# Retention and ELU layer: the opening chunks load k in one layout and get the other by transposes

## The chip, the cores and the metric

The kernel runs on one core of one Trainium2 chip. The metric is device time in microseconds (us) for one whole execution, inputs in device memory to outputs in device memory; lower is better. Lines written L307 and the like are lines of the kernel before.

## The reference

Two blocks run one after the other. The first is a retention layer with a decaying state per head (batch 4, 8 heads, 768 tokens, head size 64). The second is a two-layer network with an ELU between the layers (3072 tokens, 512 to 2048 to 512). All data is float32.

```python
for t in range(S):
    state = gamma * state + einsum('bhd,bhe->bhde', k[:, :, t], v[:, :, t])
    y[:, :, t] = scale * einsum('bhd,bhde->bhe', q[:, :, t], state)
x = y.transpose(0, 2, 1, 3).reshape(B * S, H * D)
h = x @ w_in
g = where(h > 0, h, exp(minimum(h, 0)) - 1)
out = g @ w_out
```

## The kernel before

**Tiling.** Tokens are cut into 24 chunks of 128. Four chunks make a block of 512 tokens, and there are six blocks. Within a chunk the retention is worked out in two halves of 64 tokens: products of q and k inside each half (scores), a lower-triangular mask over them, products of the masked scores with v (the inner part of the output), the state after each half (products of k and v, summed up), and products of q with the state (the part across halves). Powers of each head's decay are put on v beforehand and on the output afterwards, so the state itself needs no decay. The network then runs on a whole block. Block 0 uses plain products for its first layer (`plain_first`); later work uses Strassen products.

**Four parts of a chunk.** A chunk is one tile of 128 x 2048 numbers (1 MB). Columns 0 to 511 hold q with head dimension on the partitions, columns 512 to 1023 hold k in the same turned layout, columns 1024 to 1535 hold k with tokens on the partitions, and columns 1536 to 2047 hold v with tokens on the partitions. Scores read both turned parts. The state products read k with tokens on the partitions, so k is loaded twice. The masked scores overwrite the turned k (`mask_pair`, L328). The sums of states overwrite the other k (`state`, `state_sum`, L348 and L350).

**Weights.** They come in pieces of 1 MB in 64-bit form (`load_piece`, L142). ScalarE makes the first step of their conversion (`prepare`: L164, L166 and, unless VectorE does it, L168), VectorE the rest (`decode`: L191 and L194, after L190 where VectorE does that step too). Piece 0 becomes the first quarter of `w_a`, piece 1 the first quarter of `w_b`, piece 2 the second quarter of `w_a`. Each of the first two is handled in two halves, and a call of `take()` issues one step of a half: a half of piece 0 takes two calls.

**Order.** Every engine runs its instructions in the order in which the program issues them; nothing is reordered by a planner. Semaphore waits are inserted by the framework from the tiles that are read and written. All loads go through SyncE's queue, in this order at the start: chunk 0 first half, chunk 0 second half, piece 0 first half, chunk 1, piece 0 second half, piece 1, chunk 2, chunk 3, piece 2. The load of piece 2 waits for a GpSimd copy (L115) that waits for piece 1.

**The opening**, from L1106 on, is written out by hand:

1. TensorE multiplies zeros (`unread`, one of 512 columns, then 28 of 64), as it does later with the other calls of `unread`. Nothing reads these results.
2. Chunk 0: scores (L307), v scaled (`scale_v`, L281), mask (L328), state products (L338), state (L348), inner output (L394), the part across halves (L409, with a tiny copy `seen`, L426, between its two orders), and the output times decay powers into `xb` (L433).
3. An `unread` of 512 columns, then the scores of chunk 1.
4. ScalarE prepares piece 0, and between its two halves fills the table of decay powers for tokens 256 to 767 (`powers_of`, L249, four instructions).
5. VectorE decodes the first half of piece 0, then scales v of chunk 1 and masks its scores.
6. TensorE runs the first layer on chunk 0 (`plain_first`, L497, first part), then the state products, inner output and across part of chunk 1; VectorE sums the states between.
7. An `unread` of 512 columns, `xb` for chunk 1, decode of the second half of piece 0, decode of piece 1, and the first layer on both chunks (L497), followed by chunks 2 and 3 and the rest of the network.

`warm` and `other` are two banks of PSUM, called `pa` and `pb` in the profile.

Of the kernel before, what the change touches and what calls it, by code (L numbers as in the profile page):

```python
# [14 lines left out]
ALU = mybir.AluOpType  # L15
# [3 lines left out]
def kernel(  # L19
# [32 lines left out]
    nc = tc.nc  # L52
    PSUM = bass.MemoryType.PSUM
    P = nc.NUM_PARTITIONS
# [3 lines left out]
    C = P  # L58
# [37 lines left out]
    chunks = [divmod(m, NCH) for m in range(NCHUNK)]  # L96
    raw = {}

    def load(m, parts=1):

        if m >= NCHUNK:
            return
        t = ldpool.tile([P, 2048], FP32, name="chunk", tag="chunk")
        raw[m] = (
            t[:, 0:1024].rearrange("p (a h c) -> p a h c", a=2, c=C),
            t[:, 1024:2048].rearrange("p (a h d) -> p a h d", a=2, d=D),
        )
        for part in range(parts):
            c = slice(part * 2048 // parts, (part + 1) * 2048 // parts)
            nc.sync.dma_start(t[:, c], qkv[m, :, c])  # L110

    def hold(t, other):

# [66 lines left out]
    def decode(fine=False):  # L180

        n = len(decoded)
        if n >= NPIECE:
            return
        dst, todo = prepared[n]
        decoded.append(dst.rearrange("p (a b) -> p a b", a=2))
        vec = nc.vector
        for c, flat, hi in todo:
            if hi is not None:
                vec.tensor_scalar(c.bitcast(FP32), hi.bitcast(FP32), 2.0**-112, None, ALU.mult)  # L190
            vec.tensor_scalar(c, c, 3, 0x7FFFFFF8, ALU.logical_shift_left, ALU.bitwise_and)  # L191
            if fine:
                yield
            vec.tensor_tensor(out=flat, in0=c, in1=flat, op=ALU.add)  # L194
# [28 lines left out]
    for h in range(H):  # L223
# [10 lines left out]
    nc.gpsimd.affine_select(  # L234
        out=causal, in_=causal, compare_op=ALU.is_gt, fill=1.0, base=0, pattern=[[-1, P]], channel_multiplier=1
    )
    cmask = const.tile([P, D], FP32, name="cmask")
    for sub in range(2):
        r = slice(sub * D, (sub + 1) * D)
# [6 lines left out]
    def powers_of(tokens):  # L246
        for a in range(2):
            for u in range(2):
                nc.scalar.activation(etab[:, a, u, tokens], post[:, tokens], AF.Exp, scale=lny[:, a, u : u + 1])  # L249

    powers_of(slice(0, 2 * C))

    load(0, 2)
    parts = load_piece_parts(2)
    next(parts)
    load(1)
    next(parts, None)
    load_piece()
    load(2)
# [15 lines left out]
    def scale_v(m, by_vector=False):  # L275
        if m >= NCHUNK:
            return
        i = chunks[m][1]
        qk, kv = raw[m]
        eng = nc.vector if by_vector or m < 2 else nc.gpsimd  # L280
        eng.tensor_tensor(  # L281
            out=kv[:, 1], in0=kv[:, 1], in1=vf[:, i].unsqueeze(2).to_broadcast([C, H, D]), op=ALU.mult
        )

    rows = lambda n: slice(n * D, (n + 1) * D)
# [1 line left out]
    def state(tb, n):  # L287

        if n % (2 * CPB) == 0:
            return carry[(tb + n // (2 * CPB)) % 2]  # L290
        if (tb, n) == (0, 3):

            return xt[0].rearrange("p a t -> p (a t)")[:, 0:256].rearrange("p (h e) -> p h e", e=D)

        k = raw[tb * CPB + (n - 1) // 2][1][:, 0].rearrange("p h d -> p (h d)")
# [6 lines left out]
    def score_products(sc, tb, pp, x):  # L302
        qk = raw[tb * CPB + 2 * pp + x][0]
        for p in range(HP):
            for sub in range(2):
                for a in range(2):
                    nc.tensor.matmul(  # L307
                        sc[a][rows(sub), x, p, :], lhsT=qk[rows(a), 1, p, rows(sub)],
                        rhs=qk[rows(a), 0, p, rows(sub)], start=True, stop=True, skip_group_check=True,
                    )  # L310
# [13 lines left out]
    def mask_pair(sc, x):  # L324

        place = raw[x][0][:, 1].rearrange("p h c -> p (h c)").rearrange("p (a n t) -> p a n t", a=2, t=D)
        for a in range(2):
            nc.vector.tensor_tensor(  # L328
                out=place[:, a], in0=sc[a][:, x], in1=cmask.unsqueeze(1).to_broadcast([P, HP, D]), op=ALU.mult
            )  # L330

    def state_products(kvs, tb, pp, x, subs):
        kv = raw[tb * CPB + 2 * pp + x][1]
        for p in range(HP):
            for sub in subs:
                for a in range(2):
                    if not fresh(tb, 4 * pp + 2 * x + sub + 1):
                        nc.tensor.matmul(  # L338
                            kvs[sub][rows(a), x, p, :], lhsT=kv[rows(sub), 0, 2 * p + a, :],
                            rhs=kv[rows(sub), 1, 2 * p + a, :], start=True, stop=True, skip_group_check=True,  # L340
                        )

    def state_sum(kvs, tb, pp, x, sub, copy=None):
        n = 4 * pp + 2 * x + sub
        if fresh(tb, n + 1):
            return
        if fresh(tb, n):
            (copy or nc.scalar.copy)(state(tb, n + 1), kvs[sub][:, x])  # L348
        else:
            nc.vector.tensor_tensor(out=state(tb, n + 1), in0=kvs[sub][:, x], in1=state(tb, n), op=ALU.add)  # L350
# [38 lines left out]
    def within(tb, pp, x, j, y, pt):  # L389
        kv = raw[tb * CPB + 2 * pp + x][1]  # L390
        a, u = divmod(j, 2)
        for sub in range(2):
            for c in range(2):
                nc.tensor.matmul(  # L394
                    y[sub][rows(c), j, x, :], lhsT=kv[rows(sub), 1, head(a, u, c), :], rhs=pt(2 * u + c)[rows(sub)],
                    start=(x == 0 and j == 0), stop=False, skip_group_check=True,
                )

# [702 lines left out]

    warm, other = (bank(x).rearrange("p a b -> p (a b)") for x in "ab")

    def unread(count, n):
        for _ in range(count):
            nc.tensor.matmul(warm[:, 0:n], lhsT=blank[:, 0:P], rhs=blank[:, 0:n], start=True, stop=True, skip_group_check=True)  # L1106

    unread(1, TB)
    for n in range(28):
        nc.tensor.matmul(  # L1110
            (warm, other)[n % 2][rows(n // 2 % 2), 0:D], lhsT=blank[rows(n % 2), 0:D], rhs=blank[rows(n % 2), 0:D],
            start=True, stop=True, skip_group_check=True,
        )
    sc = [ps_r.tile([P, 2, HP, D], FP32, name="sc", tag="r") for _ in range(2)]
    score_products(sc, 0, 0, 0)
    scale_v(0)
    mask_pair(sc, 0)
    unread(1, TH)
# [369 lines left out]
```

## Time and profile before

| what | value |
|---|---|
| time, median of 3 runs | 632.92 us (632.59 to 634.07) |
| the profiled execution: its time | 632.87 us |
| its span | 630.9 us |
| TensorE matmul busy | 624.8 us, 99% of the span |
| VectorE busy | 483.1 us, 77% |
| ScalarE busy | 253.3 us, 40% |
| GpSimd busy | 21.8 us, 3% |

The span runs from the first to the last instruction of the profiled execution; its own time is 1.97 us longer. In the profile, PE is TensorE's matmul side and PEld its weight load side, DVE is VectorE, ACT is ScalarE, POOL is GpSimd, SP is SyncE. A float32 matmul leaves two records, each with its own weight load, so 16 score products of one chunk are 32 records. A row of the timeline has the start, the time it covers, the engine, the line, the operation, and output and inputs with their shapes; in brackets stands the idle time before it and what ended that. The end of a matmul record is modelled and includes the time the result takes to come out, so records of neighbouring matmuls overlap.

### The profile page before, as it was taken

To read this page: it belongs to the slowest core of one execution; us is meant where nothing else is said; L and a number is where in the kernel's file an instruction comes from. 1 tells how busy PE (TensorE), PEld (TensorE's weight loads), DVE (VectorE), ACT (ScalarE), POOL (GpSimd) and SP (SyncE) were. 2 spreads that over 40 slices of the span, in tenths; PEclk is the share of its full clock that TensorE was granted. 3 is DMA by queue.
4 is the path that set the end of the run, shared out by engine and by line. 5 is a ranking of instruction groups with operands and counts; after the bars stand their busy time and mean duration, and the time that the engine had idled before them with its cause. 6 is when DMAs were issued, how large, how long until landed. Compare 5 with 4: busy or idle time off the path is not lost.

```text
span 630.9 us, 16128 instructions
## 1 busy us (share of the span) xinstructions
PE 624.8 (99%) x6680; PEld 560.1 (89%) x6680; DVE 483.1 (77%) x884; ACT 253.3 (40%) x472; POOL 21.8 (3%) x25
## 2 busy tenths in 40 slices
PE   8999999999999999999999999999999999999998
PEld 5864578888899999889999989999988999988997
DVE  5779789989789675699685588777489877558975
ACT  6698635015541114653112646111465211366311
POOL 1021000000000000200000200000110000000000
PEclk9999999999999999999999999999999999999999
DMA  8698669689287888405888702888810798600794
GB/s 331 278 406 291 188 210 268 196 267 316 81 311 248 239 255 299 180 2 174 274 266 292 282 2 64 264 284 296 310 73 12 216 308 252 217 18 2 232 309 162
DMA packets 75897, 136.85 MB, mean 217 GB/s; under 512 B 6320, under 2 KB 31792, under 8 KB 70704
## 3 DMA queue, kind: packets, MB, share of 16 engines
q1 hardware_dynamic: 75824, 135.82, 64.8%
q8 instruction: 53, 0.87, 0.5%
q14 instruction: 20, 0.16, 0.1%
HBM read 114.56 MB, written 21.23 MB: 215 GB/s over the span
## 4 chain that ended last, share of the span: by engine, by line
PE 77%; SPq 1%; DVE 1%; DMA 1%; issue 0%; ACT 0%; ACTq 0%; DVEq 0%
PE pa L955 20%; PE pa L913 10%; PE pd L955 10%; PE pb L955 5%; PE pa L867 5%; PE pb L913 4%; PE pa L740 4%; PE qa L913 3%; PE pd L867 2%; PE qd L913 2%; PE pd L913 2%; PE pd L740 2%; PE y L394 1%; PE sc L307 1%; PE y L409 1%; PE kv L338 1%
## 5 line engine op out<-in xcount | busy, mean ns | idle before, releaser
L963 ACT COPY ms<-pa 128x128 f32<-128x128 f32 x104 | 27.7, 266 | 146.7 <-PE pa L955 146.7
L955 PE MATMUL pa<-ts,wq 128*128 128x128 f32 x560 | 74.2, 275 | 0.0
L955 PE MATMUL pd<-ts,wq 128*128 128x128 f32 x552 | 73.5, 276 | 0.0
L955 PEld LDWEIGHTS pa<-ts,wq 128*128 128x128 f32 x560 | 68.5, 192 | 0.4
L955 PEld LDWEIGHTS pd<-ts,wq 128*128 128x128 f32 x552 | 67.1, 192 | 0.6 <-DVE res L967 0.2
L955 PE MATMUL pa<-gC,wq 128*128 128x128 f32 x480 | 64.7, 278 | 0.0
L478 ACT ACTIVATE r<-r 128x512 f32<-128x512 f32 x96 | 60.5, 630 | 3.1
L955 PEld LDWEIGHTS pa<-gC,wq 128*128 128x128 f32 x480 | 59.0, 192 | 1.5 <-issue 0.3
L477 ACT ACTIVATE r<-gC 128x512 f32<-128x512 f32 x64 | 39.9, 624 | 32.4 <-DVE gC L921 32.4
L967 DVE TENSOR_TENSOR res<-pd,ms 128x128 f32<-128x128 f32 x68 | 19.5, 287 | 39.6 <-PE pd L955 38.4
L481 DVE SCALAR_TENSOR_TENSOR gC<-r,gC 128x512 f32<-128x512 f32 x64 | 44.0, 719 | 0.7 <-ACT r L478 0.7
L829 DVE TENSOR_TENSOR ts<-gC,ts 128x512 f32<-128x512 f32 x60 | 41.3, 688 | 1.0
L829 DVE TENSOR_TENSOR ts<-gC 128x512 f32<-128x512 f32 x60 | 41.0, 684 | 0.0
L281 POOL TENSOR_TENSOR chunk<-chunk,vf 128x512 f32<-128x512 f32 x16 | 20.0, 1251 | 428.8 <-DMA chunk<-in_qkv_dram 345.8
L955 PE MATMUL pb<-gC,wq 128*128 128x128 f32 x240 | 31.7, 275 | 0.0
L988 ACT COPY res<-pa 128x128 f32<-128x128 f32 x34 | 9.0, 266 | 55.0 <-PE pa L955 55.0
L955 PEld LDWEIGHTS pb<-gC,wq 128*128 128x128 f32 x240 | 29.2, 192 | 0.0
L690 ACT COPY m<-pa 128x512 f32<-128x512 f32 x24 | 13.9, 581 | 30.2 <-PE pa L740 16.3
L921 DVE TENSOR_TENSOR gC<-qa,gC 128x512 f32<-128x512 f32 x8 | 5.5, 692 | 25.0 <-PE qa L913 18.3
L913 PE MATMUL pa<-xt,w_b 128*128 128x256 f32 x96 | 23.0, 382 | 0.0
L913 PE MATMUL pa<-xt,w_s 128*128 128x256 f32 x96 | 23.0, 382 | 0.0
L913 PE MATMUL pa<-xb,w_a 128*128 128x256 f32 x96 | 22.7, 379 | 0.0
(255 smaller groups left out, 1244.3 us busy)
## 6 DMA issues: line engine op xcount, KB each, us to landing
wq<-scratch_dram SPq DMA_DIRECT2D x277, 256.0 KB, 4.3
chunk<-in_qkv_dram SPq DMA_DIRECT2D x23, 1024.0 KB, 8.6
wraw<-in_w_dram SPq DMA_DIRECT2D x15, 1024.0 KB, 6.0
out_dram<-res SPq DMA_DIRECT2D x14, 256.0 KB, 3.8
scratch_dram<-gT SPq DMA_DIRECT2D x12, 256.0 KB, 4.3
scratch_dram<-m SPq DMA_DIRECT2D x12, 192.0 KB, 6.0
scratch_dram<-so SPq DMA_DIRECT2D x4, 512.0 KB, 4.6
scratch_dram<-wi SPq DMA_DIRECT2D x2, 1024.0 KB, 6.4
```

The costliest lines, as they stand in the source:

```text
L281: eng.tensor_tensor(out=kv[:, 1], in0=kv[:, 1], in1=vf[:, i].unsqueeze(2).to_broadcast([C, H, D]), op=ALU.mult)
L477: nc.scalar.activation(e, h, AF.Relu, scale=-1.0)
L478: nc.scalar.activation(e, e, AF.Exp, scale=-1.0)
L481: nc.vector.scalar_tensor_tensor(g, e, -1.0, h, ALU.add, ALU.max)
L690: nc.scalar.copy(m, ps)
L740: nc.tensor.matmul(ps[:, fi, :], lhsT=w[:, fi, j2, :], rhs=x[:, j2, :], start=(begin and fi == 0 and j2 == 0), stop=(j2 == 1), skip_group_ ...
L829: sub = lambda o, x, y: nc.vector.tensor_tensor(out=o, in0=x, in1=y, op=ALU.subtract)
L867: nc.tensor.matmul(ps[:, f, :], lhsT=lhs[f], rhs=xs[j][k], start=(begin and f == 0), stop=True, skip_group_check=True,)
L913: nc.tensor.matmul(ps[:, fi, :], lhsT=w[:, fi, j2, :], rhs=x[:, j2, :], start=(j in (1, 7) and fi == 0 and j2 == 0), stop=(j2 == 1), skip_ ...
L955: nc.tensor.matmul(ps, lhsT=w[:, f, :], rhs=ts[j][k][:, f, :], start=(begin and f == 0), stop=(f == 3), skip_group_check=True,)
L963: nc.scalar.copy(m, ps)
L967: nc.vector.tensor_tensor(out=o, in0=x, in1=y, op=ALU.add)
```

## The change

The plain part of a chunk swaps its order on the host: v now takes columns 1024 to 1535, k with tokens on the partitions 1536 to 2047. All indices of the two follow.

For chunks 0 and 1 the last 512 columns are not loaded. Chunk 0 comes as 1024 and 512 columns (it was 1024 and 1024), chunk 1 as 1536 (it was 2048). Their k with tokens on the partitions is made on the core: four transposes on TensorE per chunk (`turn`, one per pair of heads, against an identity matrix that GpSimd builds with two new instructions) into the bank `warm`, and one ScalarE copy of 128 x 512 from there into columns 1536 to 2047 (`turned`).

In the opening, 28 multiplications of zeros become 24. The transposes of a chunk follow its scores. The `unread` of 256 columns now stands between the transposes of chunk 0 and its state products and writes `other`; the `unread` of 512 columns ahead of the scores of chunk 1 is gone. On VectorE the scaling and masking of chunk 1 come ahead of the decode of piece 0's first half, and so does the state after chunk 0; that decode now stands between `seen` and `xb` of chunk 1. The first part of the first layer moves behind the last `unread`. On ScalarE the copy `turned` of chunk 1 takes the place of `powers_of` between the halves of piece 0, and `powers_of` comes after piece 1.

```diff
-    def load(m, parts=1):
+    def load(m, cuts=(0, 2048)):
...
-        for part in range(parts):
-            c = slice(part * 2048 // parts, (part + 1) * 2048 // parts)
-            nc.sync.dma_start(t[:, c], qkv[m, :, c])
+        for lo, hi in itertools.pairwise(cuts):
+            nc.sync.dma_start(t[:, lo:hi], qkv[m, :, lo:hi])
...
+    identity = begin[:, 2 * S + P : 2 * S + 2 * P]
+    nc.gpsimd.memset(identity, 0.0)
+    nc.gpsimd.affine_select(
+        out=identity, in_=identity, compare_op=ALU.not_equal, fill=1.0, base=0, pattern=[[-1, P]], channel_multiplier=1
+    )
...
-    load(0, 2)
+    load(0, (0, 1024, 1536))
     parts = load_piece_parts(2)
     next(parts)
-    load(1)
+    load(1, (0, 1536))
...
+    def turn(m, ps):
+
+        for p in range(HP):
+            nc.tensor.transpose(ps[:, p * P : (p + 1) * P], raw[m][0][:, 1, p, :], identity)
+
+    def turned(m, ps):
+
+        nc.scalar.copy(raw[m][1][:, 1].rearrange("p h d -> p (h d)"), ps)
+
...
     unread(1, TB)
-    for n in range(28):
+    for n in range(24):
...
     score_products(sc, 0, 0, 0)
+    turn(0, warm)
+    unread(1, TH, other)
+    turned(0, warm)
     scale_v(0)
     mask_pair(sc, 0)
-    unread(1, TH)
     kvs = [ps_r.tile([P, 2, HP, D], FP32, name="kv", tag="r") for _ in range(2)]
     state_products(kvs, 0, 0, 0, range(2))
     state_sum(kvs, 0, 0, 0, 0, nc.vector.tensor_copy)
     y = outputs_of_first()
     next(y)
     next(y)
-    unread(1, TB)
     score_products(sc, 0, 0, 1)
-    state_sum(kvs, 0, 0, 0, 1)
-    prepare(2, between=lambda: powers_of(slice(2 * C, S)))
-    piece = decode(True)
-    take()
-    take()
+    turn(1, warm)
     scale_v(1)
     mask_pair(sc, 1)
-    inner = plain_first()
-    next(inner)
+    state_sum(kvs, 0, 0, 0, 1)
+    prepare(2, between=lambda: turned(1, warm))
+    piece = decode(True)
     state_products(kvs, 0, 0, 1, range(2))
     state_sum(kvs, 0, 0, 1, 0)
     next(y)
     next(y)
+    take()
+    take()
     next(y)
     unread(1, TB)
+    inner = plain_first()
+    next(inner)
     next(y, None)
     take()
     take()
     take()
     state_sum(kvs, 0, 0, 1, 1)
     prepare(2, by_vector=True)
+    powers_of(slice(2 * C, S))
     next(inner)
...
-    plain = [x.reshape(B, H, NC, C, D).transpose(0, 2, 3, 1, 4).reshape(B * NC, C, H * D) for x in (k, v)]
+    plain = [x.reshape(B, H, NC, C, D).transpose(0, 2, 3, 1, 4).reshape(B * NC, C, H * D) for x in (v, k)]
```

More of the change, by code (lines that the diff above doesn't have):

```diff
@@ L278, in scale_v @@
         i = chunks[m][1]
-        qk, kv = raw[m]
+        v = raw[m][1][:, 0]
         eng = nc.vector if by_vector or m < 2 else nc.gpsimd
         eng.tensor_tensor(
-            out=kv[:, 1], in0=kv[:, 1], in1=vf[:, i].unsqueeze(2).to_broadcast([C, H, D]), op=ALU.mult
+            out=v, in0=v, in1=vf[:, i].unsqueeze(2).to_broadcast([C, H, D]), op=ALU.mult
         )
@@ L293, in state @@
             return xt[0].rearrange("p a t -> p (a t)")[:, 0:256].rearrange("p (h e) -> p h e", e=D)
-        k = raw[tb * CPB + (n - 1) // 2][1][:, 0].rearrange("p h d -> p (h d)")
+        k = raw[tb * CPB + (n - 1) // 2][1][:, 1].rearrange("p h d -> p (h d)")
         return k[:, (n - 1) % 2 * 256 : ((n - 1) % 2 + 1) * 256].rearrange("p (h e) -> p h e", e=D)
@@ L338, in state_products @@
                         nc.tensor.matmul(
-                            kvs[sub][rows(a), x, p, :], lhsT=kv[rows(sub), 0, 2 * p + a, :],
-                            rhs=kv[rows(sub), 1, 2 * p + a, :], start=True, stop=True, skip_group_check=True,
+                            kvs[sub][rows(a), x, p, :], lhsT=kv[rows(sub), 1, 2 * p + a, :],
+                            rhs=kv[rows(sub), 0, 2 * p + a, :], start=True, stop=True, skip_group_check=True,
                         )
@@ L394, in within @@
                 nc.tensor.matmul(
-                    y[sub][rows(c), j, x, :], lhsT=kv[rows(sub), 1, head(a, u, c), :], rhs=pt(2 * u + c)[rows(sub)],
+                    y[sub][rows(c), j, x, :], lhsT=kv[rows(sub), 0, head(a, u, c), :], rhs=pt(2 * u + c)[rows(sub)],
                     start=(x == 0 and j == 0), stop=False, skip_group_check=True,
@@ L1102, with unread @@
     warm, other = (bank(x).rearrange("p a b -> p (a b)") for x in "ab")
-    def unread(count, n):
+    def unread(count, n, to=warm):
         for _ in range(count):
-            nc.tensor.matmul(warm[:, 0:n], lhsT=blank[:, 0:P], rhs=blank[:, 0:n], start=True, stop=True, skip_group_check=True)
+            nc.tensor.matmul(to[:, 0:n], lhsT=blank[:, 0:P], rhs=blank[:, 0:n], start=True, stop=True, skip_group_check=True)
     unread(1, TB)
-    for n in range(28):
+    for n in range(24):
         nc.tensor.matmul(
```

## The prediction

> **What bounds the kernel now.** I read the page first, for the share of each engine.
>
> ```profile
> span 630.9 us, 16128 instructions
> ...
> PE 624.8 (99%) x6680; PEld 560.1 (89%) x6680; DVE 483.1 (77%) x884; ACT 253.3 (40%) x472; POOL 21.8 (3%) x25
> ```
>
> TensorE is idle for 6.1 us of 630.9. Next, the view of waits for TensorE's matmul side: who made it wait in the whole span.
>
> ```profile
> PE pa L1106 <- DVE blank L208: 1.5, 1, 1.5
> PE pd L409 <- DVE seen L426: 0.5, 2, 0.3
> PE kv L338 <- DVE chunk L281: 0.4, 1, 0.4
> PE y L409 <- DVE seen L378: 0.3, 1, 0.3
> PE pa L497 <- DVE w_a L194: 0.2, 1, 0.2
> ```
>
> All of these lie in the first 28 us, and busy time by stretch is full from 30 to 140 us. So the rest is a queue of TensorE work, and a shift of where it starts goes to the end nearly one for one. But the opening's "busy" holds multiplications of zeros, so its real waits must be read in the timeline. TensorE:
>
> ```profile
> 5.15 1.06 PE L307 MATMUL sc<-chunk 64*64 64x64 f32 x32
> 6.14 0.70 PE L1106 MATMUL pa<-blank 128*128 128x256 f32 x2
> 7.21 0.69 PE L338 MATMUL kv<-chunk 64*64 64x64 f32 x32 [0.37 <-DVE chunk L281]
> ...
> 10.66 0.69 PE L307 MATMUL sc<-chunk 64*64 64x64 f32 x32
> 11.59 1.13 PE L497 MATMUL pa<-xb,w_a 128*128 128x128 f32 x8 [0.23 <-DVE w_a L194]
> 12.65 0.69 PE L338 MATMUL kv<-chunk 64*64 64x64 f32 x32
> ...
> 18.93 1.99 PE L497 MATMUL pb<-xb,w_b 128*128 128x256 f32 x8
> ```
>
> VectorE, same view:
>
> ```profile
> 11.36 0.69 DVE L281 TENSOR_TENSOR chunk<-chunk,vf 128x512 f32<-128x512 f32 x1
> 11.96 0.75 DVE L328 TENSOR_TENSOR chunk<-sc,cmask 128x256 f32<-128x256 f32 x2
> 13.38 0.42 DVE L350 TENSOR_TENSOR xt<-kv,chunk 128x256 f32<-128x256 f32 x1 [0.66 <-PE kv L338]
> ...
> 15.10 0.42 DVE L433 TENSOR_TENSOR xb<-pb,etab 128x256 f32<-128x256 f32 x1 [0.58 <-PE pb L409]
> ...
> 18.19 0.69 DVE L194 CUSTOM_DVE_ANT_0 w_b<-wraw,w_b 128x1024 uint16<-128x1024 uint16 x1
> ```
>
> (In that last row the first half of w_b is finished, at 18.88.) Chunk 1's scores wait for its load (10.66); the first layer waits for w_a, then the state products start at 12.65. From 15.10 VectorE has no gap that matters until 18.88, when TensorE can begin with w_b (18.93). After that TensorE is nearly without a gap. The opening thus ends at that 18.93, reached through 12.65.
>
> [...] No transpose is in this trace. [...] the first 32 score records take 1.06 us, the next 32 take 0.69. [...] Here the readers of successive loads start in that order, at 5.15, 6.46, 8.11, 10.66 and (piece 1) 15.06.
>
> **The change, part by part.**
>
> Loads. Chunk 0's second half took 6.46 - 5.15 = 1.31 for 512 KB; half of it saves 0.65. Chunk 1 took 10.66 - 8.11 = 2.55 for 1 MB; a quarter less saves 0.64. So v arrives at 5.81, piece 0 at 7.46, chunk 1 at 9.37, piece 1 at 13.8, piece 2 1.29 earlier than before. SyncE issues as many loads as before; the held load of piece 2 (L115) is released earlier too. [...]
>
> Transposes. Price S, first start to readable. Nearest row: eight 128x128 records take 1.13 (L497), with 0.275 for one, so each adds (1.13 - 0.275)/7 = 0.12. If a transpose leaves one record, S = 0.275 + 3 x 0.12 = 0.64, which I take. Two records each: S = 1.13[...]. [...] The copy of 128x512 from PSUM on ScalarE takes 0.58 (L690's row), with 0.05 per handoff.
>
> Chunk 0. Scores run as before, the transposes start at 6.14 and are readable at 6.78. VectorE scales v from 5.81 to 6.50. The mask overwrites the turned k, so its second half waits for all four transposes: done about 7.3 (before 7.82), harmless. Copy: 6.83 to 7.41. State products start at 7.46, where they were at 7.21 behind L281: **+0.25**. The zeros (`other`) fit into the copy's time. The chain of chunk 0 moves by 0.25, so TensorE is free at 9.51 + 0.25 = 9.76, without the `unread` that filled 9.51 to 10.64.
>
> Chunk 1. Its data is there at 9.37, so scores start at 9.76, transposes 0.56 later, the time that the weight loads of those 32 records take (10.32), readable at 10.96. ScalarE is done with piece 0's first half at 7.46 + 2.02 = 9.48, so it copies 11.01 to 11.59. VectorE leaves chunk 0 at 10.22 (9.97 + 0.25): scaling to 10.82, mask with its second half waiting for the transposes (10.96) to 11.55, then the state after chunk 0, 0.42, to 11.95. The state products write the bank that this last one reads, so beyond the first pair they wait for it, not for the copy: effective start **11.94 against 12.65, -0.71**. Queued behind it: the inner output, across part, w_a's first use.
>
> The moved decode. From the state products to the end of `seen` the sequence is the same, 1.86: 13.80 (before 14.51). In the old order the decode took 1.06 (10.30 to 11.36) ahead of the scaling; now it stands ahead of `xb`, where VectorE idled 0.58 for TensorE. So `xb` starts at 13.73 + 1.06 = 14.79 against 15.10: **-0.31**. Behind it the VectorE order is unchanged, so w_b is ready at 18.57. TensorE's side: across part done 14.25, zeros 0.86, two first-layer parts of 0.86 each and one of 1.73: 18.6 (w_a's second half, at 16.60, is in time). The two bounds agree: **-0.3**.
>
> Moved at nothing: `powers_of` (2.55) comes after piece 1 on ScalarE, 13.8 + 2.9 = 16.7 to 19.3. Its cover is ScalarE's wait of 4.87 for piece 2, now landing near 21.5; its table is first read at 27.85. If that cover went, piece 2's decode (26.95) still has slack. The first first-layer part moves behind an `unread`: counted above. GpSimd's two instructions (0.21 and 0.29 like their twins) end near 3, before 6.14. The four missing zero products (about 0.1) precede a wait for the load.
>
> Sum: 632.87 for the profiled execution (630.9 span plus 1.97 around it, untouched), minus 0.3, is **632.6**; the profiled execution lies 0.05 below the median of 632.92.
>
> Ends: [...] S = 1.13 puts scores at 10.25, transposes readable at 11.94, state at 12.75: +0.5. Loads that save only half add at most 0.3 (scores at 10.0). The first four transposes at half clock add about 0.4.
>
> **Rivals.**
>
> 1. *Transposes and copy become the wait* (a new wait for the one removed). The scores, transposes, mask and state sum stand in series, as above: S = 1.13 with slow clock or short saving, +0.5 to +1.1, 633.4 to 634.0. For it: nothing in this trace prices a transpose. Against it: two transpose groups would have to cost as much as full products.
> 2. *Slower: the clock.* Place: 6.1, where the clock has just come up, and 10.96 to 11.9, where TensorE now stands without its zeros. If the transposes don't count and the clock stays or falls to half[...], that window's work (the second chunk's products, zeros and first-layer parts, 2.3 to 3 us) takes twice its time: +2.3, about 635.2. It decides once more than 1.9 us of work on the path runs at half clock. Against it: [...] the trace kept full clock across its own waits.
> 3. *The loads were the bound, everything comes 1.29 earlier*: 631.6. Against it: VectorE's serial 1.06 decode is only moved, and TensorE's own sum reaches 18.6.
> 4. *Nothing gained*: the load is hidden, the copy eats it: 632.9.
>
> **How the numbers follow.** The forecast 0.57, rival 4 0.14, rival 1 0.18, rival 3 0.05, rival 2 0.06. A measurement of this kernel can tell about 0.3% (1.9 us) from no change; only rival 2 passes that upwards. Even rival 3 stays within it; for more than 1.9 us I know no source and leave 0.02 out of rival 3's chance. Faster 0.02, same 0.92, slower 0.06. The range holds the forecast, rivals 1 and 4, the price bounds and the runs' own spread (632.59 to 634.07): 632.0 to 634.0.
>
> **What would show it.** Right: chunk 1's scores near 9.8 without a wait for a load; state products near 12, released by VectorE's state sum after chunk 0, `xb` near 14.8, the first w_b product near 18.6. Wrong: transposes that cover over 1 us, state products of chunk 1 released by ScalarE, a second score group as slow as the first (clock), or gaps in TensorE after 19.

## The result, and the profile after

The changed kernel takes **636.3 us** (median of 7 executions, 634.94 to 638.53) against 633.01 us (7 executions, 632.59 to 634.31): ratio 1.0046, 95% interval 1.0027 to 1.0064. It is slower, by 0.46%. The forecast was 632.6 us within 632.0 to 634.0: outside, on the wrong side.

Every execution also gives TensorE's mean granted clock over the span. Four of the seven executions of the changed kernel show 0.994 or 0.995, and their median is 636.67; the other three show 1.0, median 635.35. So there are two losses: about 2.3 us that is there at full clock (635.35 - 633.01; in the second session below, where the clocks of the kernel before are on record too, it is 1.6), and more where the clock fell. The profiled execution (635.65 us, span 633.8) is one at full clock. Lines from here on are lines of the changed kernel, mostly 13 above those of before (but the scaling is L285, L281 before, and the mask L332, L328 before); experiments built on the kernel before keep its lines, and e8 and e9 have a few of their own.

The page of the changed kernel:

```profile
span 633.8 us, 16133 instructions
...
PE 624.8 (99%) x6678; PEld 560.8 (88%) x6678; DVE 483.8 (76%) x884; ACT 254.0 (40%) x474; POOL 21.0 (3%) x27
...
q8 instruction: 53, 0.87, 0.5%
```

TensorE is busy for the same 624.8 us as before; the span is 2.9 longer, all of it idle time. The view of waits says who made it wait (engine, line, what it waited for; total, times, longest):

```profile
PE pa L1119 <- DVE blank L207: 1.5, 1, 1.5
PE y L422 <- issue: 1.3, 1, 1.3
PE kv L351 <- DVE chunk L332: 0.7, 1, 0.7
PE pd L422 <- DVE seen L439: 0.5, 2, 0.3
PE pa L753 <- DVE m L608: 0.5, 1, 0.5
PE pa L753 <- ACT m L703: 0.5, 1, 0.5
```

The first and fourth were there before. The third is chunk 1's wait in the opening; the view puts it down to the mask, which is not so, as shown below. The second, fifth and sixth are new and lie far from the change: at 301.94, 134.23 and 141.92 us. The opening itself, on TensorE (start, length):

```profile
5.89 1.07 PE L339 MATMUL pa<-so,chunk 128*128 128x128 f32 x4
...
7.63 0.69 PE L351 MATMUL kv<-chunk 64*64 64x64 f32 x32 [0.24 <-ACT chunk L343]
...
10.47 0.66 PE L339 MATMUL pa<-so,chunk 128*128 128x128 f32 x4
11.80 1.20 PE L351 MATMUL kv<-chunk 64*64 64x64 f32 x29 [0.68 <-DVE chunk L332]
...
19.14 1.91 PE L510 MATMUL pb<-xb,w_b 128*128 128x256 f32 x8
...
27.57 0.67 PE L510 MATMUL hp<-xb,w_a 128*128 128x256 f32 x2
```

And on VectorE:

```profile
11.72 0.41 DVE L363 TENSOR_TENSOR chunk<-kv,chunk 128x256 f32<-128x256 f32 x1
13.08 0.42 DVE L363 TENSOR_TENSOR xt<-kv,chunk 128x256 f32<-128x256 f32 x1 [0.94 <-PE kv L351]
...
15.21 0.42 DVE L446 TENSOR_TENSOR xb<-pb,etab 128x256 f32<-128x256 f32 x1
```

State products of chunk 1 start at 11.80, but cover 1.20 where they covered 0.69. ScalarE's copy and the weight loads of these products show what they wait for:

```profile
11.16 0.58 ACT L343 COPY chunk<-pa 128x512 f32<-128x512 f32 x1 [1.69 <-PE pa L339]
```

```profile
11.80 0.20 PEld L351 LDWEIGHTS kv<-chunk 64*64 64x64 f32 x4 [0.91 <-ACT chunk L343]
12.19 0.67 PEld L351 LDWEIGHTS kv<-chunk 64*64 64x64 f32 x25 [0.20 <-DVE chunk L363]
```

The first weight load waits for a semaphore of ScalarE, so the copy, done at 11.74, releases it; the mask is no input of these products and ends at 11.81, after they have started. After the first two products, whose records start from 11.80 to 11.91, nothing starts until 12.19, when VectorE's sum of states (L363, 11.72 to 12.13) is done. A second gap, from 12.43 to 12.60, is ended by nothing that the profile shows.

`xb` comes at 15.21 (before 15.10), the first w_b product at 19.14 (18.93), and the work on `hp` at 27.57 (27.78). So at the end of the opening, at full clock, the changed kernel is ahead by no more than 0.2 us. To see where the time went, I matched TensorE's instructions of the two traces and took the median shift of after against before in stretches of before's time: -0.20 us at 27.5 to 30, 0.01 at 60 to 80 and at 110 to 130, **1.21** at 142 to 150, 1.08 at 280 to 297, **2.56** at 300 to 310, 2.56 at the end. Two steps, near 134 to 142 and near 300, make the whole loss of this execution.

**The first step, traced back.** TensorE waits at 134.23 for `m` (L608, VectorE) and at 141.92 for `m` (L703, ScalarE). Followed back, VectorE has been late since 95 us, where it makes sums of weights in the buffers of `m` and must wait until stores that read these buffers have landed in device memory. Before:

```profile
94.54 0.55 DVE L647 TENSOR_TENSOR m<-w_s 128x384 f32<-128x384 f32 x1
```

After, with a wait of 1.01 us for the stores of `m`:

```profile
95.64 0.56 DVE L660 TENSOR_TENSOR m<-w_s 128x384 f32<-128x384 f32 x1 [1.01 <-DMA scratch_dram<-m]
```

Those stores are issued by SyncE. Before:

```profile
88.32 4.30 SPq L643 DMA_DIRECT2D scratch_dram<-m  x4
```

After, starting earlier and covering 1.77 us more (6.07 - 4.30):

```profile
87.71 6.07 SPq L656 DMA_DIRECT2D scratch_dram<-m  x4
```

What else was moving then? The page's "q8 instruction" is a queue of instruction packets: 53 of 16 KB, 0.87 MB in all. The trace places each one. The reads near these stores (start in us, length in ns):

```
                before        after         one zero less (e2)   filler and count (e5)
9th read      78.94/ 880    78.63/1020      78.34/ 881           78.96/ 880
10th read     86.57/1335    92.27/ 935      92.17/ 936           86.18/1031
11th read    114.98/ 931   115.22/1195     114.61/ 931          114.75/ 938
```

The tenth read came 5.7 us later and fell among these stores. Whether that is a cause, and of what, is what half of the experiments ask.

### The profile page after: what moved, and what is told of

It reads as the page before. It is cut to its first block, busy times and chain, and to the rows that moved or that the text cites. A ratio compares the mean times of both kernels' runs of the same rounds, so it can differ in the third digit from the quotient of the medians.

```text
span 633.8 us, 16133 instructions
## 1 busy us (share of the span) xinstructions
PE 624.8 (99%) x6678; PEld 560.8 (88%) x6678; DVE 483.8 (76%) x884; ACT 254.0 (40%) x474; POOL 21.0 (3%) x27
## 4 chain that ended last, share of the span: by engine, by line
PE 77%; SPq 1%; DVE 1%; DMA 1%; issue 1%; ACT 0%; ACTq 0%; DVEq 0%
PE pa L968 20%; PE pa L926 10%; PE pd L968 10%; PE pb L968 5%; PE pa L880 5%; PE pb L926 4%; PE pa L753 4%; PE qa L926 3%; PE pd L880 2%; PE qd L926 2%; PE pd L926 2%; PE pd L753 2%; PE y L407 1%; PE y L422 1%; PE sc L311 1%; PE kv L351 1%
## 5 line engine op out<-in xcount | busy, mean ns | idle before, releaser
L285 POOL TENSOR_TENSOR chunk<-chunk,vf 128x512 f32<-128x512 f32 x16 | 18.8, 1177 | 433.8 <-DMA chunk<-in_qkv_dram 347.5
L703 ACT COPY m<-pa 128x512 f32<-128x512 f32 x24 | 13.9, 580 | 29.8 <-PE pa L753 16.0
```

The source lines that it names most:

```text
L285: eng.tensor_tensor(out=v, in0=v, in1=vf[:, i].unsqueeze(2).to_broadcast([C, H, D]), op=ALU.mult)
L703: nc.scalar.copy(m, ps)
```

## The experiments

Theory I ("blocks"): the number of instructions on TensorE ahead of a given place moved, and with it the times at which its instruction blocks are read; one read then collides with the stores near 92 us. Theory II ("clock"): without the zeros TensorE stands idle in the opening, and in part of the executions the clock falls. Rival A: the transposes do the harm to the clock, as the prediction's second rival had it. Rival B: the new waits of the opening (copy, sum of states) are passed on to the end.

A product of zeros is four instructions on TensorE (two records, each with its own weight load). "Count" below is the number of TensorE instructions ahead of the same later place, less that of the kernel before; the changed kernel stands at -3. "Step" is the loss between 110 to 130 and 142 to 150 us in the profiled execution. "Low" is the number of executions with a mean clock under 0.9985. The last column is the median of the others, and in brackets its distance to before's own at full clock in the same session (633.20, 633.92 and 633.4 us for e1 to e4, e5 to e8, e9 to e12).

| run | count | 10th read | step | low / all | full-clock median |
|---|---|---|---|---|---|
| changed, first session | -3 | 92.27 | 1.20 | 4 / 7 | 635.35 (+2.3) |
| e4 changed again | -3 | 92.94 | 1.49 | 2 / 8 | 634.79 (+1.59) |
| e1 changed, one zero more | +1 | 88.90 | 0.18 | 9 / 16 | 633.55 (+0.35) |
| e2 before, one zero less | -4 | 92.17 | 1.01 | 0 / 17 | 634.25 (+1.05) |
| e3 before, no filler | 0 | 86.29 | 0.16 | 8 / 22 | 633.18 (-0.02) |
| e5 changed, filler | +2 | 86.18 | 0.07 | 0 / 13 | 633.86 (-0.06) |
| e6 changed, filler, two zeros less | -6 | 93.07 | 1.25 | 2 / 6 | 636.49 (+2.57) |
| e7 before, one zero moved | 0 | 87.01 | -0.01 | 2 / 13 | 633.63 (-0.29) |
| e8 changed, turned by products | +1 | 88.44 | 0.20 | 4 / 14 | 635.24 (+1.32) |
| e9 before, transposes for zeros | 0 | 86.46 | -0.07 | 0 / 14 | 634.18 (+0.8) |
| e10 as e3 | 0 | 87.03 | 0.29 | 8 / 14 | 633.41 (0.0) |
| e11 before, one zero more | +4 | 90.14 | 0.08 | 2 / 14 | 633.27 (-0.1) |
| e12 changed, filler, four zeros more | +18 | 84.95 | 0.16 | 0 / 14 | 635.08 (+1.7) |

The profiled executions of e1 and e11 were low ones, whose whole timeline runs 2.7 and 4.3 us late by then; their reads lie that much later too. The profiled execution of e10 was low as well, and 0.6 late.

**e1: one zero product more in the changed kernel.**

```diff
-    for n in range(24):
+    for n in range(25):
```

> The changed kernel with 25 instead of 24 products of zeros at the start: four more TensorE instructions, one more than the kernel before has at the same later place. In the changed kernel's trace the opening ends 0.2 us earlier than before, and the loss comes in steps far from it: about 1.2 us between 88 and 140 us, 1.3 us near 300 us, each next to a 16 KB read on the instruction queue that comes late against its neighbours (92.27 instead of 86.57, 299.17 instead of 294.48). Theory I (fetch): the changed kernel has three TensorE instructions fewer, so every 16 KB block of its instructions ends three instructions later in the code, and two of these ends fall behind a semaphore wait. Then this kernel is back at the time before or 0.2 us under it: 632.5 to 633.5, ratio 0.999 to 1.001, no gap near 300. Rival (the transposes, the copy or the order cost it): no change against the changed kernel, 635 to 636.5.

Measured: 635.2 us, 16 executions, ratio 1.0022 (1.001 to 1.0034). Four useless instructions took the step away (0.18 against 1.20) and at full clock all but 0.35 us of the loss. But 9 of 16 executions were low, median 635.84, and that is what is left in the median. The profiled one was low, and shows what it looks like. Windows (stretch, its length, busy time with counts of TensorE, weight loads, VectorE, ScalarE and GpSimd, granted clock, DMA share, GB/s), e1:

```profile
12.40:19.20 6.80, 6.17 (x90) 4.84 (x91) 4.66 (x13) 5.79 (x10) 0.17 (x1) 0.51 0.99 413
```

The changed kernel's profiled execution in the same stretch:

```profile
12.40:19.20 6.80, 6.54 (x119) 5.38 (x112) 5.41 (x14) 6.42 (x10) 0.17 (x1) 1.00 1.01 417
```

The clock is 0.51 and TensorE gets through 90 matmul records instead of 119. The records of the clock give full from 5.65 us, half from 12.47 to 19.30, then full to the end; this execution leaves the opening 2.5 us late. One such stretch of 6.8 us also explains the mean: 6.8 / 2 of 634 is 0.54%, so 0.994 to 0.995. Here is what theory II expected.

**e2: one zero product less in the kernel before.** Nothing else of the change is in it.

```diff
-    for n in range(28):
+    for n in range(27):
```

> The kernel before with 27 instead of 28 products of zeros: four TensorE instructions fewer, no transposes, no other order, the same loads. Theory I (fetch): the blocks of instructions end four instructions later, about as in the changed kernel; the gap near 298 to 301 us and the late stores near 90 us appear: 635 to 635.8, ratio 1.003 to 1.005. Rival (the change itself costs it): one product of zeros less ahead of a wait for a load changes nothing, 632.6 to 633.5.

Measured: 634.25 us, 17 executions, ratio 1.0016 (1.0008 to 1.0023). At the end of its opening it is even 0.21 us ahead of before's, and then comes the step, with the late tenth read. VectorE, e2:

```profile
95.22 0.56 DVE L647 TENSOR_TENSOR m<-w_s 128x384 f32<-128x384 f32 x1 [0.83 <-DMA scratch_dram<-m]
```

And e2's waits, of which the first was below 0.2 us before and the second is new:

```profile
PE pa L740 <- ACT m L690: 0.5, 1, 0.5
...
PE pa L740 <- DVE m L595: 0.3, 1, 0.3
```

So the step does not need transposes, copies or another order: four instructions fewer are enough. The loss, 1.0 us, is half of what I had looked for, since I had expected the gap near 300 us too, and it is not in this trace.

**e3: the kernel before without its `unread` of 512 ahead of chunk 1's scores**, with one zero product more so that the count stays.

```diff
-    for n in range(28):
+    for n in range(29):
...
-    unread(1, TB)
     score_products(sc, 0, 0, 1)
```

> The kernel before without the zeros of 512 columns ahead of chunk 1's scores, and with 29 instead of 28 small ones, so that the number of TensorE instructions is the same afterwards. Four of seven executions of the changed kernel show a mean granted clock of 0.994 to 0.995, the others 1.0, and are longer by about 1 us. Theory II (clock): without these zeros TensorE stands long enough in the opening for its clock to fall[...] in some executions: some clocks of 0.995 here, and these executions 1 to 3 us longer, the others at 632.6 to 633.5. Rival (the clock falls for another reason, or falls in the kernel before too): clocks of 1.0 in all, or 0.995 as often without any cost.

Measured: 633.87 us, 22 executions, ratio 1.0014 (1.0003 to 1.0025). At full clock it is before's time; 8 of 22 executions are low (0.997), median 635.44. Without the zeros, and without a transpose, the clock falls in some executions: rival A is not needed. e10 below is the same kernel, and its profile happened to be a low one.

**e4: the changed kernel again**, beside the three above.

> The changed kernel once more, beside the others on one chip, for the spread of its times and clocks. Theory I and the rival alike: 635 to 636.5 in executions with clock 1.0, ratio 1.003 to 1.006. Theory II: about half the executions at clock 0.995, 1 to 3 us longer than the rest. If theory I holds and the gaps are fixed by the code, its trace shows the same gap near 300 and the same late stores near 92 as the first trace.

Measured: 635.59 us, 8 executions, ratio 1.0026 (1.0008 to 1.0045). The tenth read and the step are as in the first profile. The gap near 300 us is not. In the first profile of the changed kernel the products of q and the state stand still in the middle of a group:

```profile
300.17 0.52 PE L422 MATMUL y<-chunk 64*64 64x64 f32 x20
301.94 0.33 PE L422 MATMUL y<-chunk 64*64 64x64 f32 x4 [1.25 <-issue]
```

In e4, the same program, they don't:

```profile
301.78 0.63 PE L422 MATMUL y<-chunk 64*64 64x64 f32 x24
```

Its trace lost 0.7 us elsewhere, near 179 us, waiting for weights read back from memory:

```profile
PE pa L968 <- DMA wq<-scratch_dram: 0.7, 1, 0.7
```

So the second step of the first profile comes and goes from execution to execution.

**e5 and e6: the wait covered, with and without the count.** Both put a product of zeros, 384 columns into a spare bank, behind chunk 1's transposes, where TensorE stood. e5 has 24 zeros (count +2), e6 22 (count -6).

```diff
     turn(1, warm)
+    spare = bank("a").rearrange("p a b -> p (a b)")
+    unread(1, 384, spare)
     scale_v(1)
```

> The changed kernel with one product of zeros of 384 columns, into the spare bank of pa, behind the transposes of chunk 1; with the framework's waits it has two TensorE instructions more than the kernel before at the same later place. Theory I (fetch) with theory II (clock): both losses go. Clocks of 1.0 in nearly all executions, the read of instructions near 86 us on time, and what is left is the gain of 0.2 us in the opening: median 632.6 to 633.2 with a before of about 633.1, ratio 0.999 to 1.000. Rival (the transposes and the copy cost it): still 634.5 or more.

> The same filler of zeros, with 22 instead of 24 small products: six TensorE instructions fewer than the kernel before. Theory I with II: the clock stays at 1.0, but the block of instructions near 86 us is read late (near 92), and about 1.2 us (1 to 2) is lost by 141 us: median 634 to 635. If the filler alone were what counts: 632.6 to 633.2.

Measured: e5 633.86 us, 13 executions, ratio 0.9995 (0.9979 to 1.0011), none low. e6 636.86 us, 6 executions, ratio 1.0052 (1.0036 to 1.0067). The two differ by eight instructions of no use, and by 3.0 us. e5 on TensorE has the filler where the wait of 0.68 was, and VectorE is on time near 95:

```profile
10.63 0.81 PE L1119 MATMUL pa<-blank 128*128 128x384 f32 x2
11.47 0.73 PE L351 MATMUL kv<-chunk 64*64 64x64 f32 x16
12.52 0.46 PE L351 MATMUL kv<-chunk 64*64 64x64 f32 x16 [0.32 <-issue]
```

```profile
94.43 0.55 DVE L660 TENSOR_TENSOR m<-w_s 128x384 f32<-128x384 f32 x1
```

e6's waits hold the pair at `m` again, and two stands of the "issue" kind (nothing that the profile shows was waited for), one in the opening and one near 300:

```profile
PE kv L351 <- issue: 1.0, 1, 1.0
PE y L422 <- issue: 0.9, 1, 0.9
PE pa L753 <- DVE m L608: 0.6, 1, 0.6
...
PE pa L753 <- ACT m L703: 0.5, 1, 0.5
```

Rival B falls with e5: it keeps the copy, the transposes and the new order, and takes before's time. It isn't faster than before, though: the forecast gain of 0.3 us doesn't show. e6 lost more than I had expected, through those two stands. Two of its six executions are low in spite of the filler; a stand of 1.0 us is in its opening all the same (in a profiled execution that kept full clock), so that this stand lets the clock fall is only argued.

**e7: one zero product of the kernel before moved** from the opening to behind the last `unread`, so that the count is 4 lower only up to there.

```diff
-    for n in range(28):
+    for n in range(27):
...
     unread(1, TB)
+    unread(1, D)
     next(y, None)
```

> The kernel before with 27 small products of zeros at the start and one further small one at 15 to 16 us, behind the last zeros of 512 columns. Theory I: what counts is the number of TensorE instructions ahead of the code at 86 us, which is that of the kernel before: read on time, 632.6 to 633.5, ratio 0.9995 to 1.0005. Rival (the one product less at the start did it, by the clock or by timing, as in the run with 27): 634 to 634.5, ratio 1.001 to 1.002.

Measured: 633.73 us, 13 executions, ratio 1.0004 (0.9992 to 1.0017); no step, and the tenth read on time. It has one zero product less in the opening's start, as e2, without e2's loss. What matters is the count at the later place, not the missing zero at the start.

**e8: the transposes of the changed kernel as ordinary products** with the identity, count +1.

```diff
-            nc.tensor.transpose(ps[:, p * P : (p + 1) * P], raw[m][0][:, 1, p, :], identity)
+            nc.tensor.matmul(
+                ps[:, p * P : (p + 1) * P], lhsT=raw[m][0][:, 1, p, :], rhs=identity, start=True, stop=True, skip_group_check=True,
+            )
...
-    for n in range(24):
+    for n in range(21):
```

> The changed kernel with plain float32 matmuls against the identity in place of the transposes, and 21 small products of zeros, so that it has one TensorE instruction more than the kernel before. If the clock falls because transposes do not count as activity: it now stays, clocks of 1.0 in nearly all executions. If it falls because TensorE stands without zeros from 11 to 12 us: 0.994 to 0.997 in a third or more, as before. In executions at full clock the time is 632.8 to 633.8: the eight products take about 0.5 us longer per chunk than the transposes, of which some shows.

Measured: 635.7 us, 14 executions, ratio 1.0032 (1.0018 to 1.0046); full-clock 635.24, where I expected 632.8 to 633.8: a miss. TensorE, e8:

```profile
10.97 1.16 PE L339 MATMUL pa<-so,chunk 128*128 128x128 f32 x8
...
14.42 0.46 PE L353 MATMUL kv<-chunk 64*64 64x64 f32 x16 [1.00 <-issue]
```

Four ordinary products leave eight records and cover 1.16 us; four transposes leave four and cover 0.66. A stand of 1.0 us inside the state products comes on top, and the opening ends 1.6 us late. 4 of 14 executions are low, against 6 of 15 with transposes (after and e4): ordinary products don't keep the clock up either, and so few executions can't tell the two apart.

**e9: transposes in place of zeros.** In the kernel before, the `unread` of 512 becomes eight transposes of the blank tile; 25 zeros keep the count.

```diff
-    for n in range(28):
+    for n in range(25):
...
-    unread(1, TB)
+    for n in range(8):
+        nc.tensor.transpose(warm[:, n % 4 * P : (n % 4 + 1) * P], blank[:, 0:P], identity)
     score_products(sc, 0, 0, 1)
```

> The kernel before with eight transposes that nothing reads (about 0.9 us, an identity built on GpSimd) in place of the zeros of 512 columns ahead of chunk 1's scores, and 25 instead of 28 small products of zeros: the same number of TensorE instructions afterwards. TensorE is as busy there as in the kernel before. If transposes count as activity for the clock: clocks of 1.0 as in the kernel before (2 of 51 lower), ratio 0.999 to 1.001. If they do not: lower clocks in a third of the executions, as without the zeros (8 of 22), these 2 us longer; the rest at the time before.

Measured: 634.18 us, 14 executions, ratio 1.0003 (0.999 to 1.0015). The eight fill the place that the zeros filled:

```profile
9.09 1.09 PE L1131 MATMUL pa<-so,blank 128*128 128x128 f32 x8
```

None of 14 executions is low. With nothing in that place (e3 and e10) 16 of 36 were. In this place, between other products, transposes keep the clock up as zeros do; this goes against the prediction's second rival. Whether they would bring a slow clock up is not tested. The full-clock median is 0.8 above before's while the profiled execution is 0.2 ahead; that difference stays unexplained.

**e10: e3's kernel again**, in e9's session.

> The kernel before without the zeros of 512 columns and with 29 small ones, again, on the chip of the run with transposes in their place: clocks of 0.997 in about a third of the executions, these about 2 us longer, the others as the kernel before.

Measured: 633.8 us, 14 executions, ratio 1.0005 (0.9986 to 1.0023); 8 low, six of 0.997 and two of 0.994. Now one program shows both. TensorE in e3, at full clock:

```profile
10.35 0.69 PE L307 MATMUL sc<-chunk 64*64 64x64 f32 x32 [1.08 <-DMA chunk<-in_qkv_dram]
...
12.34 0.69 PE L338 MATMUL kv<-chunk 64*64 64x64 f32 x32
```

And in e10, where the clock records give half speed from 11.48 to 14.89, 3.41 us:

```profile
10.40 0.69 PE L307 MATMUL sc<-chunk 64*64 64x64 f32 x32 [1.23 <-DMA chunk<-in_qkv_dram]
...
12.89 1.13 PE L338 MATMUL kv<-chunk 64*64 64x64 f32 x32
```

Windows, e10:

```profile
11.48:14.89 3.41, 3.41 (x84) 3.19 (x86) 1.25 (x4) 2.78 (x6) 0.00 (x0) 0.50 1.01 425
```

The wait is nearly the same, 1.08 and 1.23 us; one execution falls and the other doesn't. Nor is the cost always the same: e10's low executions have a median of 634.58, 1.2 above its others, e3's are 2.3 above. The clock records hold a hint at what decides. In each of the three profiles that caught a fall (e1, e10, e11) it comes 6.83 us after the clock rose, and the clock had risen at 5.64, 4.65 and 5.01 us; in the four profiles with the place unfilled that kept full clock (after, e3, e4, e8) it rose at 5.74 to 6.86. That the moment of the rise decides is suggested by these few, not shown.

e10's profile also holds the gap near 300 (1.8 us) with a count of 0, so that gap is not fixed by the count.

**e11: one zero product more in the kernel before** (29).

```diff
-    for n in range(28):
+    for n in range(29):
```

> The kernel before with 29 instead of 28 small products of zeros: four TensorE instructions more, so every block of instructions ends four instructions earlier in the code. Theory I: a block that ends ahead of the wait near 86 us still ends ahead of it, so nothing is lost there: 0.9995 to 1.0005 of the kernel before. Rival (any shift of the blocks costs 1 us): 1.001 or more.

Measured: 633.47 us, 14 executions, ratio 0.9996 (0.9982 to 1.001), no step. Before does not sit on a lucky number: four more do no harm, four fewer (e2) do. Two executions are low although the zeros ahead of chunk 1's scores are there. The profiled one is one of them, and its load came late:

```profile
PE sc L307 <- DMA chunk<-in_qkv_dram: 1.7, 1, 1.7
```

**e12: e5 with 28 zeros**, count +18.

```diff
-    for n in range(24):
+    for n in range(28):
```

> The changed kernel with the filler of 384 columns and 28 instead of 24 small products of zeros: 18 TensorE instructions more than the kernel before. In the version with filler and 24, TensorE still lost 0.3 us inside chunk 1's state products to a block of instructions that was not there; here that block is asked for earlier. Theory I: that gap is smaller, the read near 86 us on time, clock 1.0, 632.2 to 632.9 against a before of 633.1, ratio 0.9985 to 0.9995, if no other block comes to lie behind a wait; if one does, 1.001 to 1.002.

Measured: 635.08 us, 14 executions, ratio 1.0015 (1.0003 to 1.0027), none low. Not e5's time: no step near 134, but waits of the "issue" kind that e5 doesn't have, at 24 and 221 us:

```profile
PE pd L510 <- issue: 0.5, 1, 0.5
PE pb L968 <- issue: 0.4, 1, 0.4
```

The stand inside chunk 1's state products, 0.3 us in e5, is gone, as expected, and the read on time. But the count is no simple knob: with this number TensorE stands in other places. No kernel here beats before; e5 equals it.

**The "issue" stands, all together.** In the 14 traces (before, after and e1 to e12) I looked for every stand of TensorE after the first 5 us that is longer than 0.15 us and that no semaphore wait ends. There are twelve: inside chunk 1's state products (e1, e4, e5, e6, e8, e9), near 300 us (after, e6, e10), at 32.3 in e11, and e12's two. Each of them ends between 1.27 and 1.57 us after a 16 KB read of instructions has landed. So I read these as waits for instructions. In e12 the first read begins at 8.83 us, in the six with the stand in the opening at 10.02 to 12.03. The gap near 300 goes with the 25th read: it begins at 299.17, 300.66 and 300.32 where the gap is, at 292.9 to 298.2 elsewhere (299.07 in e11, whose timeline is late).

**What follows.** In the 13 profiles of the table, the tenth read is late and the step at least 1.0 us in all four with a count of -3 to -6 (after, e4, e2, e6), and in none of the nine with 0 or more (at most 0.29). e2 against before and e5 against e6 change nothing but such instructions. That the number of TensorE's instructions decides the first step is shown.

That the late read delays the stores is read from the trace: in each of these four, the one store whose issue the read falls on takes about 1 us longer (the fourth of `m` 3.56, 3.91 and 3.74 us in after, e4 and e6, against 2.0 to 2.7 in the others; in e2 the first of `gT`, 1.49 against 0.5 to 0.6). The rest of the 1.77 between before and after is spread that comes without a late read too: the four stores cover 4.92 in e5. When the tenth read begins, TensorE has started 2455 to 2462 of its instructions in the nine profiles and in before, 2507 to 2512 in the four. Why three fewer make that difference no trace shows; theory I's blocks that end behind a waiting instruction are my guess.

For the clock, the change's own form without filler has 19 low of 45 (after, e4, e1, e8), e5 and e12 with filler 0 of 27, but e6, with the same filler, 2 of 6; before had 7 of 129 over the three sessions.

Open: why the 25th read, and with it the gap near 300 us, comes late in some executions (after, e6, e10) and not in others, the same program among them (e4); the wait for `wq` near 179 (0.7 in e4); and the differences at full clock that no step explains (e9, part of e8 and of e12).

## Why the prediction was wrong

**Loads: right.** v is scaled at 5.57 (forecast 5.81), and piece 2 is taken up by ScalarE at 21.80 (about 21.5).

**Transposes and copy: right.** S = 0.64 was taken; chunk 1's four cover 0.66, in one record each. The 0.275 in it is what the trace of before shows for one 128x128 record of a product (L497, 275 ns). The records of these four float32 transposes are 272 to 329 ns long and start 0.11 us apart (forecast 0.12): the estimate held for transposes as well, which nothing in the trace of before assured, so that is partly luck. The first four, which started at 5.89, before the clock records begin with full clock (6.78), covered 1.07 and cost little: state products of chunk 0 at 7.63 for 7.46. Rival 1 did not happen.

**Chunk 1, +0.25 then -0.71: the start right, the length mis-sized.** Scores at 9.79 to 9.90 (forecast 9.76), transposes 10.47 (10.32), copy at 11.16 (11.01), state products at 11.80, released by ScalarE's copy, which the prediction had named as a sign of being wrong. That holds for the first two products only: the others waited for the sum of states, as forecast, but it ended at 12.13, not at 11.95, and they start at 12.19 (forecast: all effectively from 11.94). A second gap, 12.43 to 12.60, was not in the forecast at all: it ends 1.4 us after the first read of instructions landed (10.28 to 11.19), as the "issue" stands of 0.3 to 1.0 us at the same place do in e1, e4, e5, e6 and e8. `xt` is 0.30 earlier (13.08 for 13.38) where the forecast needed 0.71.

**The moved decode: the working right, its input wrong.** It takes 1.07 ahead of `xb` (forecast 1.06) and eats 0.41 of the lead (forecast 0.71 - 0.31 = 0.40), so 0.30 ahead becomes 0.11 behind, at 15.21, where the same sum on 0.71 gave 14.79. The w_b product follows at 19.14, forecast 18.6. Only at 27.57 is the kernel 0.20 ahead.

**`powers_of` at nothing: right.** 2.54 us, followed by a wait of 2.79 for piece 2.

**"The four missing zero products (about 0.1) precede a wait for the load": wrong.** Costed as time at their place, they are free. But they take 16 instructions off a count that ends at -3, and e1 shows that one of them put back takes the step of 1.2 us away. This is the first step that failed: a term put at nothing measured 1.2 us, far from its place. I had not looked at the instruction queue on the page, and held "a shift of where it starts goes to the end nearly one for one" without asking what else moves with the program.

**Rival 2, given 0.06: it happened, in 6 of 15 executions.** This is the second step that failed. Place and size were there: TensorE stands before 12 us, falls to half for a stretch (granted clock 0.50 for 3.41 us in e10, 0.51 over 6.8 us in e1), and e1's and e3's low executions cost 2.3 us, the forecast's +2.3; the changed kernel's own cost 1.3 (636.65 against 635.33). Three things were wrong. That the pause is about 1 us long was no reason against: e10 shows the fall with a wait of 1.23. "The trace kept full clock across its own waits" rested on a single execution; before itself falls in 7 of 129. And the cause was sought in the transposes, for which the trace of before, having none, shows nothing. e9 disagrees: 0 of 14 low. The cause is the removed zeros, as e3 and e10 show without a transpose: 16 of 36 low. The amount of work that the forecast's +2.3 puts at half clock was my estimate; the trace of before shows no such fall.

**The sum.** 632.6 was forecast, 636.3 measured, 3.3 above before. At full clock +2.3, of which 1.2 is the step (the late tenth read); 1.5 came in the profiled execution from the gap near 300 (the late 25th), which e4, at +1.6, does not have. The forecast's -0.3 came out as -0.2 at the end of the opening, and was gone by 60 us (0.01). The rest is the clock: four of those seven executions fell, so the median lies among them. Of the signs of being wrong that the prediction named, the last came true as well: gaps in TensorE after 19 (at 134, 142 and 302 us).

## What to carry to other kernels

Before removing "useless" work from a kernel that TensorE bounds, ask what it holds up besides time: the clock (16 of 36 executions low in e3 and e10; look at the mean clock of many executions, not at one profile) and the times at which the instruction blocks are read. A change of a few instructions at the start can cost a microsecond far away (the step of 1.01 in e2); test it by adding or removing idle instructions alone, in both kernels, and compare the traces' shift along the whole span. Where a stand in the opening can't be avoided, try to fill it, with zeros or transposes alike (e5, e9), and count the instructions that this adds (e6, e12).

## What the runs showed of the hardware

- Packets of instructions, 53 of 16 KB in each of before and after, come on a DMA queue of their own (q8), 0.88 to 1.62 us each. Twelve times in 14 traces TensorE stands ("issue", 0.25 to 1.8 us) until 1.3 to 1.6 us after such a read has landed.
- A read of instructions that fell on the stores near 92 us lengthened one store's issue by about 1 us, in four profiles of four. This is no rule: on many other issues of these traces a read falls without any delay, on nearly all of the loads of weight pieces for instance.
- The clock fell to half for 3.41 us (e10, granted 0.50, after a stand of 1.23 us; e11, in one of 1.67) or for 6.83 us (e1, granted 0.51 over 12.40 to 19.20, with stands of 0.68 and 0.42 us near it), in some executions only: 16 of 36 without filler in before's form. In these three profiles it fell 6.83 us after it had risen.
- Four float32 transposes of 128x128 leave four records and cover 0.66 us (after); as ordinary products they leave eight and cover 1.16 (e8). Eight transposes in place of the zeros hold the clock (e9: 0 of 14 low).
